# Two more weight pieces prepared ahead of the first step, rows copied ahead of the activation tables, reciprocals half a step later

## The chip, the cores and the metric

The kernel runs on one core of a Trainium2 chip. The metric is the device time of one execution in microseconds (us), lower is better. In the names used here PE is TensorE (matrix multiplies; PEld is its weight load), ACT is ScalarE, DVE is VectorE, POOL is GpSimd, and SP is the engine that issues the DMAs. Each engine works through its own queue in the order in which the program wrote it.

## The reference

Attention with two kinds of windows feeds a gated feed-forward layer. Only the shape of the work matters here:

```python
# q, k, v: batch 8, heads 8, seq 576, head_dim 64
scores = scale * q @ k.T            # masked to a window of 32 keys (plain, or every 4th key)
attn   = exp(scores - max) / (sum + 1e-9)
x      = attn @ v                   # as 4608 tokens x 512
h      = x @ w_in                   # 512 x 2048
sp     = max(h, 0) + log1p(exp(-abs(h)))
out    = (h * erf(sp)) @ w_out      # 2048 x 512
```

`w_in` and `w_out` come in as 64-bit numbers. The kernel turns each into a high and a low 32-bit part.

## The kernel before

**Attention units.** The attention is cut into 72 units of four blocks. Unit n passes through: `scores(n)` (PE), `mask_max(n)` (DVE: mask and row maximum), `exponents(n)` (four exponentials with row sums on ACT, then one small addition to the sums on POOL, line 207), `normalize(n)` (a reciprocal on DVE, then a multiplication of the unit's probabilities on POOL, line 212), `transposes(n)` (PE, line 217), `turned(n)` (a copy of the turned probabilities out of PSUM, line 220), `values(n)` (PE, line 233), `rows_hi(n)` (ACT casts the result into x's high part, line 266) and `rows_lo(n)` (DVE subtracts to get x's low part, line 271). A unit is transposed three units after it is scored (`LAG = 3`).

**Weights.** A piece of weights is loaded by a DMA, then passes ACT (`prep_act`, lines 369 and 374) and DVE (`prep_dve`, lines 383 to 389) over several calls. One call works on several pieces at once: on ACT a cast and one activation, on DVE four operations.

**Two parts.** First 14 visits, n = 0 to 13, run attention alone: visit n scores unit n and transposes unit n - 3 (`first_visit`). In visits 1 to `EARLY` a call on the weights goes along, and there the copy `turned` is on ACT; in the other visits it is on DVE. Then come steps t of two half steps x = 2t and 2t + 1. Each half step has `mm1` (PE, twelve 128x512 multiplies into `h`, line 446), `take` (DVE copies `h`), and from t = 2 also `mm2` (PE, twelve multiplies into `acc`, line 487) for the step two before. On ACT the odd half steps run `argument(t)` (sigmoid and logarithm with table loads, lines 458 and 459) and `table(t-1)` (erf, line 462). In x = 0 to 6 one unit n = 14 + x is scored in each half step and unit n - 3 = 11 + x is transposed. While t < 2 the transposes stand ahead of `mm1` in PE's queue; `values` and `scores` stand behind it.

All queues are written out by hand (a manual schedule): what the code says first on an engine runs first there.

Of the kernel before, what the change touches and what calls it, by code (L numbers as in the profile page):

```python
# [10 lines left out]
F32 = mybir.dt.float32  # L11
# [7 lines left out]
P = 128  # L19
# [15 lines left out]
PER = 4  # L35
# [18 lines left out]
SPC = FT // PAIR  # L54
# [5 lines left out]
USED = {p: min(t for t, (_, q, _) in enumerate(STEPS) if q == p) for p in range(SPC)}  # L60

LAG = 3
FIRST = NBLK + LAG + 2

FREE = FIRST - LAG + 4

EARLY = 9

SAVED = 2 * (HALF + 1) + 1

# [42 lines left out]
def attn_moe_kernel(ctx: ExitStack, tc: tile.TileContext, qk, v, masks, eye, w_in, w_out, out):  # L113
# [3 lines left out]
    def pool(name, bufs, space=bass.MemoryType.SB, **kw):  # L117
        return ctx.enter_context(tc.tile_pool(name=name, bufs=bufs, space=space, **kw))
# [7 lines left out]
    io, work, small = pool("io", 2), pool("work", 2), pool("small", 3)  # L126
# [47 lines left out]
    probs, maxes, sums, x_rows = {}, {}, {}, {}  # L174
# [3 lines left out]
    def scores(u):  # L178
        i = u % 2
        for j in range(PER):  # L180
            at, r = QW + key_start(u, j), j % 2 * BLK
            for h in range(2):
                hs = slice(h * D, (h + 1) * D)
                nc.tensor.matmul(sps[h][r:r + BLK, i, j // 2, :], qkz[i][hs, j * BLK:(j + 1) * BLK],  # L184
                                 qkz[i][hs, at:at + KEYS], start=True, stop=True)

    def mask_max(u):
        pr = probs[u] = work.tile([P, PER, KEYS], F32, name="prob", bufs=LAG + 1)
        nmax = maxes[u] = small.tile([P, PER], F32, name="nmax")
        for h in range(2):  # L190
            for p in range(PER // 2):
                n = PER * u + 2 * p
                nc.vector.tensor_tensor_reduce(  # L193
                    out=pr[:, 2 * h + p, :], in0=sps[h][:, u % 2, p, :], in1=mask[PAIRS.index((kind(n), kind(n + 1)))],
                    scale=-SCALE, scalar=BIG,
                    op0=ALU.add, op1=ALU.min, accum_out=nmax[:, 2 * h + p:2 * h + p + 1],
                )

    def exponents(u):
        nmax = maxes.pop(u)  # L200
        sums[u] = small.tile([P, PER], F32, name="ssum")
        for j in range(PER):
            nc.scalar.activation(  # L203
                out=probs[u][:, j, :], in_=probs[u][:, j, :], func=AF.Exp,
                scale=-1.0, bias=nmax[:, j:j + 1], accum_out=sums[u][:, j:j + 1],
            )
        nc.gpsimd.tensor_scalar(sums[u], sums[u], 1.0e-9, None, op0=ALU.add)

    def normalize(u):
        rinv = small.tile([P, PER], F32, name="rinv")  # L210
        nc.vector.reciprocal(out=rinv, in_=sums.pop(u))
        nc.gpsimd.tensor_tensor(probs[u], probs[u], rinv.broadcast_to([P, PER, KEYS]), op=ALU.mult)
# [9 lines left out]
    def turn(units):  # L222
        for u in units:
            transposes(u)
        for u in units:
            turned(u, nc.vector.tensor_copy)

    def values(u):
        xp, vt, pt = place(u), vz[u % 2], pz[u in second]
        for j in range(PER):  # L230
            r = j % 2 * BLK
            for h in range(2):
                nc.tensor.matmul(xp[h * D:(h + 1) * D, j * BLK:(j + 1) * BLK], vt[:, j, h, :],  # L233
                                 pt[:, 2 * h + j // 2, r:r + BLK], start=True, stop=True)

    def pieces(u):

# [26 lines left out]
    def rows_hi(u):  # L264
        for hi, _, src in rows_of(u):
            nc.scalar.copy(out=hi, in_=src)  # L266
# [27 lines left out]
    def has(u):  # L294
        return 0 <= u < NU

    def first_visit(n):

        m = n - LAG
        copy = nc.scalar.copy if 1 <= n <= EARLY else nc.vector.tensor_copy  # L300
        if has(m):
# [3 lines left out]
        if has(m):  # L305
            turned(m, copy)
        if 1 <= n <= EARLY:
            prep_act()
# [68 lines left out]
    def prep_dve(keep=None):  # L377

        if rest and rest[0][0] < calls[0]:
            _, w, hi, lo = rest.popleft()
            nc.vector.tensor_tensor(lo, w, hi.bitcast(F32), op=ALU.subtract)  # L383
        if begun and begun[0][0] < calls[0]:
            _, i, d, hi, lo, w = begun.popleft()
            t = w.bitcast(I32)
            nc.vector.tensor_scalar(t, t, 3, None, op0=ALU.logical_shift_left)
            nc.vector.scalar_tensor_tensor(t, d[:, :, 1], -0x80000000, t, op0=ALU.bitwise_and, op1=ALU.bitwise_or)  # L388
            nc.vector.scalar_tensor_tensor(t, d[:, :, 0], 29, t, op0=ALU.logical_shift_right, op1=ALU.bitwise_or)  # L389
            made.append((w, hi, lo))  # L390
            if i != keep:
                soon(load_w, i)
# [68 lines left out]
    def table(t):  # L461
        nc.scalar.activation(out=ls[t], in_=ls[t], func=AF.Erf, scale=-1.0)  # L462
# [66 lines left out]
    with tc.manual_schedule():  # L529
        load_qk(0)  # L530
        nc.sync.dma_start(out=cst, in_=masks)
        for t in vz:
            nc.gpsimd.memset(t[KEYS:P], 0.0)
        nc.gpsimd.memset(pz[0][KEYS:P], 0.0)
        load_qk(1)
        nc.sync.dma_start(out=ident, in_=eye)
        for n in range(FIRST):
            if n < 3:
                load_w(n)
            first_visit(n)  # L540
            if 1 <= n <= EARLY:
                prep_dve()
        normalize(FIRST - 2)
        rows_lo(FIRST - 1 - LAG)

        plan = visits()

        pause = 2 * (USED[SPC - 1] + 1) - 2

        late = 3  # L550
        todo, scaled = [], [FIRST - 1]
        for x in range(2 * (NT + 2)):
            t, j = divmod(x, 2)
            ns = plan.get(x, [])
            scored, ready = [n for n in ns if has(n)], [n - LAG for n in ns]
            second.update(ready[1:])

            if t < 2:
                turn(ready)
            if t < NT:  # L560
                after = STEPS[t + 1][0] if ends(t) and t + 1 < NT else None
                if x == 2 * HALF - 4:
                    load_x(1, range(twice))
                elif after and after > 1 and j == 0:
                    load_x(after, range(twice))
                if x in (2 * HALF - 2, SAVED):
                    hold(True)
                mm1(t, j)
                if x == 0:
                    for a in stores:  # L570
                        store_x(*a)
                if after is not None and j == PAIR - 1:
                    load_x(after, range(twice, CC))
                    hold(False)
                take(t, j)

            if j == 0 and x or x == 1:
                for u in todo:
                    exponents(u)
                scaled, todo = scaled + todo, []  # L580
            if j == 1 and 1 <= t <= NT:
                table(t - 1)
            if t >= 2:
                turn(ready)
            if j == 1 and 1 <= t <= NT:
                gate(t - 1, 0)
            if j == 0 and 2 <= t:
                gate(t - 2, 1)
            if j == 1 and t < NT:
                argument(t)  # L590
            if x != pause:
                prep_act()
            if x not in (pause, late):
                prep_dve(keep=2 if SAVED - 4 < x <= SAVED else None)
            if t >= 2:
                mm2(t - 2, j)
                if x == SAVED:
                    save()
                    hold(False)
                    load_w(2)  # L600
                elif ends(t - 2):
                    if j == 1:
                        store(STEPS[t - 2][0])
                    elif STEPS[t - 2][2] == 2:
                        fetch()
            for m in ready:
                values(m)
            for n in scored:
                scores(n)
            for n in ns:  # L610
                soon(load_qk, n + 2)
                soon(load_v, n - 1)
            for n in scored:
                mask_max(n)
                todo.append(n)
            if x == late:
                prep_dve()
            while scaled:
                normalize(scaled.pop(0))
            for m in ready:  # L620
                rows_hi(m)
            for m in ready:
                rows_lo(m)
            if x == SAVED + 2:
                nc.gpsimd.memset(pz[1][KEYS:P], 0.0)
        assert not todo and not prep and not staged and not begun and not made and not rest
# [84 lines left out]
```

## Time and profile before

| | |
|---|---|
| median of 3 runs | 943.51 us (941.78 to 943.67) |
| the profiled execution | 942.44 us, of which 940.7 us lie between its first and last instruction (the span) |
| PE busy in the span | 915.1 us, 97% |
| ACT, DVE, POOL busy | 642.5, 562.2, 82.9 us |
| mean granted TensorE clock | 0.997 of full speed |

Times of trace rows are microseconds from the span's start. A row of the timeline gives the start, the duration, the engine, the line and the operation; in brackets stands how long the engine had been idle and what it waited for.

### The profile page before, as it was taken

The numbers are of one execution on the slowest core, as the hardware profiler recorded it, in microseconds if no ns is written. First come the engines' busy times: TensorE is split into PE (matmuls) and PEld (weight loads), VectorE is DVE, ScalarE is ACT, GpSimd is POOL, SyncE is SP. The second block draws the span as 40 slices with busy tenths as digits, with TensorE's granted clock in tenths as the row PEclk, the third lists the DMA queues.
The fourth block names the chain that finished last, engine by engine and source line by source line (L and its number), as shares of the span: only waits on it lengthen the run. The fifth ranks groups of instructions, "written<-read, shape, count | busy, mean of one in ns | idle before, by whom it ended". The sixth has DMA issues, their size and how long they took to land.

```text
span 940.7 us, 15969 instructions
## 1 busy us (share of the span) xinstructions
PE 915.1 (97%) x6048; PEld 747.8 (80%) x6048; DVE 562.2 (60%) x1511; ACT 642.5 (68%) x1202; POOL 82.9 (9%) x154
## 2 busy tenths in 40 slices
PE   5789999999999999999999999999999999999998
PEld 4567887888888878888888878888888888888886
DVE  6879889886565545555665555555555444335434
ACT  7879888785866866667578657866566555445553
POOL 2321110110100100000000000100000000000000
PEclk9999999999999999999999999999999999999999
DMA  8766444432631242313232152314220302011001
GB/s 277 254 219 222 155 155 136 156 112 94 194 111 67 67 157 67 111 68 116 83 111 73 62 186 103 112 60 132 84 78 34 114 12 79 1 45 45 0 1 45
DMA packets 51500, 98.73 MB, mean 105 GB/s; under 512 B 7136, under 2 KB 20192, under 8 KB 51424
## 3 DMA queue, kind: packets, MB, share of 16 engines
q1 hardware_dynamic: 51136, 97.19, 30.9%
q8 instruction: 48, 0.79, 0.3%
q10 hardware_dynamic: 288, 0.52, 0.1%
q14 instruction: 28, 0.23, 0.1%
HBM read 69.52 MB, written 27.26 MB: 103 GB/s over the span
## 4 chain that ended last, share of the span: by engine, by line
PE 88%; DVE 6%; DMA 3%; ACT 2%; issue 1%; POOL 0%; SPq 0%; POOLq 0%; ACTq 0%; DVEq 0%
PE h L446 40%; PE acc L487 39%; PE tx L233 3%; PE sp L184 3%; PE sp L217 3%; DMA x<-xT 1%; DVE w L388 1%; DVE w L389 1%; DMA qk<-in_qk_dram 1%; DVE prob L193 1%; DVE win_lo L383 1%; PE acc L217 1%; DVE s L469 1%; DMA dbl<-in_w_in_dram 0%; DVE pT L220 0%
## 5 line engine op out<-in xcount | busy, mean ns | idle before, releaser
L454 DVE COPY hc<-h 128x512 f32<-128x512 f32 x144 | 99.5, 691 | 273.5 <-PE h L446 273.1
L446 PE MATMUL h<-x,win_hi 128*128 128x512 f32 x832 | 259.3, 393 | 0.9 <-DMA x<-xT 0.9
L487 PE MATMUL acc<-wout_hi,ghi 128*128 128x512 f32 x576 | 227.5, 395 | 1.2 <-DVE rows L271 1.0
L487 PE MATMUL acc<-wout_lo,ghi 128*128 128x512 f32 x576 | 224.4, 390 | 0.0
L458 ACT ACTIVATE s<-hc 128x1024 f32<-128x1024 f32 x72 | 76.4, 1062 | 184.4 <-DVE hc L454 184.3
L446 PEld LDWEIGHTS h<-x,win_hi 128*128 128x128 f32 x832 | 155.0, 188 | 35.2 <-issue 1.4
L446 PE MATMUL h<-x,win_lo 128*128 128x512 f32 x416 | 162.3, 390 | 0.0
L487 PE MATMUL acc<-wout_hi,glo 128*128 128x512 f32 x576 | 158.8, 389 | 0.0
L487 PEld LDWEIGHTS acc<-wout_hi,ghi 128*128 128x128 f32 x576 | 108.2, 188 | 23.6 <-DVE rows L271 1.4
L487 PEld LDWEIGHTS acc<-wout_hi,glo 128*128 128x128 f32 x576 | 108.1, 188 | 22.6
L487 PEld LDWEIGHTS acc<-wout_lo,ghi 128*128 128x128 f32 x576 | 108.3, 188 | 21.4
L203 ACT ACTIVATE prob<-prob,nmax 128x96 f32<-128x96 f32 x288 | 104.0, 364 | 5.4 <-DVE nmax L193 5.1
L473 DVE TENSOR_TENSOR glo<-s,ghi 128x512 fp32r<-128x512 f32 x144 | 99.7, 693 | 5.1
L459 ACT ACT_TABLE_LOAD x72 | 92.4, 1283 | 1.3
L462 ACT ACT_TABLE_LOAD x72 | 92.4, 1283 | 1.3
L469 DVE TENSOR_TENSOR s<-hc,s 128x1024 f32<-128x1024 f32 x72 | 88.1, 1224 | 7.1 <-ACT s L462 7.1
L446 PEld LDWEIGHTS h<-x,win_lo 128*128 128x128 f32 x416 | 78.3, 188 | 16.7
L193 DVE CUSTOM_DVE_ANT_0 prob<-sp,cst 128x96 f32<-128x96 f32 x288 | 54.8, 253 | 51.8 <-PE sp L184 51.7
L446 PE MATMUL h<-dbl,win_hi 128*128 128x512 f32 x256 | 80.7, 396 | 0.0
L266 ACT CAST rows<-tx 128x64 fp32r<-128x64 f32 (+5 forms) x116 | 26.2, 356 | 75.2 <-PE tx L233 75.2
L462 ACT ACTIVATE s<-s 128x1024 f32<-128x1024 f32 x72 | 76.5, 1062 | 0.8
L459 ACT ACTIVATE s<-s 128x1024 f32<-128x1024 f32 x72 | 76.4, 1061 | 0.8
(59 smaller groups left out, 929.2 us busy)
## 6 DMA issues: line engine op xcount, KB each, us to landing
xT<-rows SPq DMA_DIRECT2D x26, 576.0 KB, 4.7
v<-in_v_dram SPq DMA_DIRECT2D x72, 192.0 KB, 3.8
qk<-in_qk_dram SPq DMA_DIRECT2D x48, 272.0 KB, 3.9
dbl<-in_w_in_dram SPq DMA_DIRECT2D x16, 512.0 KB, 4.2
dbl<-in_w_out_dram SPq DMA_DIRECT2D x16, 512.0 KB, 3.4
qk<-in_qk_dram SPq DMA_DIRECT2D x24, 288.0 KB, 3.9
out_dram<-w SPq DMA_DIRECT2D x26, 256.0 KB, 2.3
x<-xT SPq DMA_DIRECT2D x8, 320.0 KB, 5.2
```

The lines of the kernel that those rows point to most:

```text
L184: nc.tensor.matmul(sps[h][r:r + BLK, i, j // 2, :], qkz[i][hs, j * BLK:(j + 1) * BLK], qkz[i][hs, at:at + KEYS], start=True, stop=True)
L193: nc.vector.tensor_tensor_reduce(out=pr[:, 2 * h + p, :], in0=sps[h][:, u % 2, p, :], in1=mask[PAIRS.index((kind(n), kind(n + 1)))], scale ...
L203: nc.scalar.activation(out=probs[u][:, j, :], in_=probs[u][:, j, :], func=AF.Exp, scale=-1.0, bias=nmax[:, j:j + 1], accum_out=sums[u][:, ...
L217: nc.tensor.transpose(out=turn_place(u)[0:KEYS, j * P:(j + 1) * P], in_=pr[:, j, :], identity=ident)
L446: nc.tensor.matmul(h, w[:, cc, ft * P:(ft + 1) * P], x[cc], start=(k == 0 and i == 0), stop=(k == CC - 1 and i == 2))
L454: nc.vector.tensor_copy(out=hs[t][:, j], in_=h)
L458: nc.scalar.activation(out=ls[t], in_=hs[t], func=AF.Sigmoid, scale=-1.0)
L459: nc.scalar.activation(out=ls[t], in_=ls[t], func=AF.Ln, bias=TINY)
L462: nc.scalar.activation(out=ls[t], in_=ls[t], func=AF.Erf, scale=-1.0)
L469: nc.vector.tensor_tensor(out=e, in0=hc, in1=e, op=ALU.mult)
L473: nc.vector.tensor_tensor(out=glo, in0=e[:, j], in1=ghi.bitcast(F32), op=ALU.subtract)
L487: nc.tensor.matmul(acc[tt], g[:, tt * P:(tt + 1) * P], w[:, ft, :], start=(first and w is wout_hi and g is ghi), stop=(last and g is glo))
```

## The change

`EARLY` goes from 9 to 11, so visits 10 and 11 each get a call on the weights, and their `turned` copy moves from DVE to ACT. In return half steps 2 and 3 have no such call. In the half steps before t = 2, `values`, `scores` and `rows_hi` are written ahead of `argument` and `prep_act` (`attend`). `normalize` of a unit whose exponentials were issued in half step x is written in half step x + 1, behind `take` and ahead of `gate`, unless its transposes come in x + 1: then it stays at the end of x. Two small buffers get one more copy.

```diff
-EARLY = 9
+EARLY = 11
...
-        sums[u] = small.tile([P, PER], F32, name="ssum")
+        sums[u] = small.tile([P, PER], F32, name="ssum", bufs=LAG + 1)
...
+    def attend(ready, scored):
+        for u in ready:
+            values(u)
+        for u in scored:
+            scores(u)
+        for u in ready:
+            rows_hi(u)
...
-        pause = 2 * (USED[SPC - 1] + 1) - 2
-        late = 3
-        todo, scaled = [], [FIRST - 1]
+        pause = 2, 3, 2 * (USED[SPC - 1] + 1) - 2
+        due = {n - LAG: x for x, ns in plan.items() for n in ns}
+        todo, scaled, fresh = [], [FIRST - 1], []
...
-                scaled, todo = scaled + todo, []
+                fresh, todo = todo, []
             if j == 1 and 1 <= t <= NT:
                 table(t - 1)
+            if t < 2:
+                attend(ready, scored)
             if t >= 2:
                 turn(ready)
+            while scaled:
+                normalize(scaled.pop(0))
+            scaled, fresh = fresh, []
...
-            if x != pause:
+            if x not in pause:
                 prep_act()
-            if x not in (pause, late):
                 prep_dve(keep=2 if SAVED - 4 < x <= SAVED else None)
...
-            for m in ready:
-                values(m)
-            for n in scored:
-                scores(n)
+            if t >= 2:
+                attend(ready, scored)
...
-            if x == late:
-                prep_dve()
-            while scaled:
-                normalize(scaled.pop(0))
-            for m in ready:
-                rows_hi(m)
+            for u in [u for u in scaled if due[u] == x + 1]:
+                scaled.remove(u)
+                normalize(u)
             for m in ready:
                 rows_lo(m)
```

Three places show the move in the queues. The first is POOL's queue from the last visit to half step 3. Line 207 is the addition to a unit's sums and line 212 the multiplication of its probabilities; the tile numbers of before are prob_666, 708, 778 and 846 for units 12, 13, 14 and 15, whose sums for 14 and 15 are ssum_811 and 877. Before:

```order
L212 TENSOR_TENSOR prob_666<-prob_666,rinv_723 128x384
L212 TENSOR_TENSOR prob_708<-prob_708,rinv_784 128x384
L207 TENSOR_SCALAR ssum_811<-ssum_811 128x4
L212 TENSOR_TENSOR prob_778<-prob_778,rinv_852 128x384
L207 TENSOR_SCALAR ssum_877<-ssum_877 128x4
L212 TENSOR_TENSOR prob_846<-prob_846,rinv_916 128x384
```

In the changed kernel the same units are prob_684, 726, 802 and 865, and the sums of 14 and 15 are ssum_829 and 892:

```order
L212 TENSOR_TENSOR prob_684<-prob_684,rinv_741 128x384
L212 TENSOR_TENSOR prob_726<-prob_726,rinv_788 128x384
L207 TENSOR_SCALAR ssum_829<-ssum_829 128x4
L207 TENSOR_SCALAR ssum_892<-ssum_892 128x4
L212 TENSOR_TENSOR prob_802<-prob_802,rinv_917 128x384
L212 TENSOR_TENSOR prob_865<-prob_865,rinv_969 128x384
```

The multiplication of unit 14 stood ahead of the addition of unit 15 and now stands behind it.

The second place is ACT's queue from the exponentials of unit 14 to those of unit 15 (half steps 1 and 2). `rows` is x's part, `s` and `hc` belong to `argument(0)`, `wout_hi` and `w` to the weights. Before:

```order
L203 ACTIVATE prob_778,ssum_811<-prob_778,nmax_779 128x96 x4
L458 ACT_TABLE_LOAD
L458 ACTIVATE s_749<-hc_748 128x1024
L459 ACT_TABLE_LOAD
L459 ACTIVATE s_749<-s_749 128x1024
L369 CAST wout_hi_82<-w_516 128x512
L374 ACTIVATE w_820<-dbl1_552 128x512
L266 CAST rows_788<-acc1_94 128x256
L203 ACT_TABLE_LOAD
L203 ACTIVATE prob_846,ssum_877<-prob_846,nmax_847 128x96 x4
```

In the changed kernel:

```order
L203 ACTIVATE prob_802,ssum_829<-prob_802,nmax_803 128x96 x4
L274 CAST rows_786<-acc1_94 128x256
L466 ACT_TABLE_LOAD
L466 ACTIVATE s_767<-hc_766 128x1024
L467 ACT_TABLE_LOAD
L467 ACTIVATE s_767<-s_767 128x1024
L377 CAST wout_hi_82<-w_622 128x512
L382 ACTIVATE w_855<-dbl0_657 128x512
L203 ACT_TABLE_LOAD
L203 ACTIVATE prob_865,ssum_892<-prob_865,nmax_866 128x96 x4
```

The cast of x's part (unit 12) moved ahead of `argument(0)`; the exponentials of unit 15 stay behind `argument(0)` and the call on the weights.

The third place is PE's queue at the start of half step 3, in the changed kernel: the transposes of unit 14 (prob_802), then `mm1`, then `values(14)`.

```order
L217 MATMUL acc3_96<-ident_58,prob_802 96x128 x4
L454 MATMUL h_109<-x0_97,win_hi_80 128x512 x2
L454 MATMUL h_109<-x0_97,win_lo_81 128x512
L454 MATMUL h_109<-x1_98,win_hi_80 128x512 x2
L454 MATMUL h_109<-x1_98,win_lo_81 128x512
L454 MATMUL h_109<-x2_99,win_hi_80 128x512 x2
```

Nothing moved here: PE's queue holds the same operations in the same order in both kernels, from the first to the last.

## Rows read from the trace of the kernel before

**Rows 1.** Busy time by stretch: length, PE, PEld, DVE, ACT, POOL, clock, DMA.
```profile
0.00:49.60 49.60, 34.27 (x447) 25.16 (x448) 37.50 (x179) 37.57 (x151) 14.75 (x32) 1.00 0.78 259
49.60:90.00 40.40, 35.54 (x317) 27.28 (x316) 33.47 (x101) 35.20 (x82) 8.03 (x11) 0.96 0.67 224
90.00:941.00 851.00, 845.27 (x5287) 695.39 (x5285) 491.23 (x1233) 569.70 (x972) 60.14 (x111) 1.00 0.27 90
```

**Rows 2.** Timeline, half steps 1 to 3, all engines.
```profile
57.60 0.69 PE L233 MATMUL acc<-pT,v 128*64 128x64 f32 x16 [0.51 <-DVE pT L220]
57.63 1.28 ACT L458 ACT_TABLE_LOAD   x1
...
63.33 0.36 ACT L266 CAST rows<-acc 128x256 fp32r<-128x256 f32 x1
...
64.79 0.69 PE L233 MATMUL acc<-pT,v 128*64 128x64 f32 x16 [2.71 <-DVE pT L220]
...
66.25 1.09 PE L217 MATMUL acc<-ident,prob 128*96 128x128 f32 x4
...
66.44 0.60 ACT L369 CAST wout_hi<-w 128x512 fp32r<-128x512 f32 x1
...
70.77 0.69 PE L233 MATMUL acc<-pT,v 128*64 128x64 f32 x16
```

**Rows 3.** Busy time by stretch, PE's low clock (columns as in Rows 1).
```profile
66.00:68.00 2.00, 2.00 (x16) 1.55 (x12) 1.93 (x8) 2.00 (x8) 0.76 (x1) 0.50 0.05 12
68.00:70.00 2.00, 2.00 (x9) 1.61 (x8) 1.58 (x10) 1.97 (x3) 0.83 (x1) 0.81 0.57 215
```

**Rows 4.** PE's waits, 60 to 90 us: total, times, longest.
```profile
PE acc L487 <- DVE rows L271: 1.0, 1, 1.0
PE sp L217 <- POOL prob L212: 0.7, 1, 0.7
```

**Rows 5.** Timeline, visits 9 and 10.
```profile
34.25 0.57 ACT L220 COPY pT<-acc 96x512 f32<-96x512 f32 x1
34.34 0.17 DVE L211 RECIPROCAL rinv<-ssum 128x4 f32<-128x4 f32 x1
...
34.88 1.12 PE L233 MATMUL acc<-pT,v 128*64 128x64 f32 x16 [0.68 <-ACT pT L220]
...
35.77 0.67 DVE L383 TENSOR_TENSOR win_lo<-w,win_hi 128x512 fp32r<-128x512 f32 x1
...
37.62 0.37 ACT L203 ACTIVATE prob<-prob,nmax 128x96 f32<-128x96 f32 x1
...
38.15 0.68 DVE L220 COPY pT<-acc 96x512 f32<-96x512 f32 x1
...
38.88 1.12 PE L233 MATMUL acc<-pT,v 128*64 128x64 f32 x16 [0.55 <-DVE pT L220]
```

**Rows 6.** Timeline of PE, visits 11 to 13 and half step 0.
```profile
40.49 1.09 PE L217 MATMUL acc<-ident,prob 128*96 128x128 f32 x4 [0.48 <-POOL prob L212]
...
41.50 0.92 PE L184 MATMUL sp<-qk 64*64 64x96 f32 x16
...
46.80 0.64 PE L217 MATMUL acc<-ident,prob 128*96 128x128 f32 x4 [0.83 <-POOL prob L212]
...
49.28 0.64 PE L217 MATMUL acc<-ident,prob 128*96 128x128 f32 x4 [0.38 <-POOL prob L212]
49.65 0.30 PEld L446 LDWEIGHTS h<-x,win_hi 128*128 128x128 f32 x2
...
52.59 0.69 PE L233 MATMUL acc<-pT,v 128*64 128x64 f32 x16
```

**Rows 7.** Timeline of DVE and POOL, last visit and half step 0.
```profile
49.19 0.16 DVE L211 RECIPROCAL rinv<-ssum 128x4 f32<-128x4 f32 x1
...
50.92 0.22 POOL L207 TENSOR_SCALAR ssum<-ssum 128x4 f32<-128x4 f32 x1 [1.70 <-ACT prob L203]
...
51.22 0.83 POOL L212 TENSOR_TENSOR prob<-prob,rinv 128x384 f32<-128x384 f32 x1
```

More of the change, by code (lines that the diff above doesn't have):

```diff
@@ L188, in mask_max @@
         pr = probs[u] = work.tile([P, PER, KEYS], F32, name="prob", bufs=LAG + 1)
-        nmax = maxes[u] = small.tile([P, PER], F32, name="nmax")
+        nmax = maxes[u] = small.tile([P, PER], F32, name="nmax", bufs=LAG + 1)
         for h in range(2):
@@ L575, in attn_moe_kernel @@
                 take(t, j)
-            if j == 0 and x or x == 1:
+            if x == 1 or j == 0 and x:
                 for u in todo:
                     exponents(u)
-                scaled, todo = scaled + todo, []
+                fresh, todo = todo, []
             if j == 1 and 1 <= t <= NT:
                 table(t - 1)
+            if t < 2:
+                attend(ready, scored)
             if t >= 2:
                 turn(ready)
+            while scaled:
+                normalize(scaled.pop(0))
+            scaled, fresh = fresh, []
             if j == 1 and 1 <= t <= NT:
```

## The prediction

> **What bounds the kernel now.** I first read the busy times by stretch [rows 1]. From 90 us to the end PE is busy 845.27 of 851.00 us: there the kernel is bound by PE, and since the change leaves PE's queue as it is, operation for operation, nothing can be won or lost there except by a new wait. The time that can move lies ahead of 90 us: PE is idle 15.3 us in the visits (49.60 - 34.27) and 4.9 us in the first half steps (40.40 - 35.54). So the forecast is the answer to one question: how much earlier or later does PE come out of this stretch?
>
> The timeline shows the largest wait of the half steps [rows 2]. `argument(0)` starts on ACT at 57.63, and with the call on the weights behind it holds ACT until 63.33. Only then comes the cast of x's part of unit 12. DVE's subtraction needs it, the copy of the next unit's turned probabilities is queued behind that subtraction, and `values(13)` on PE starts at 64.79 after 2.71 us idle. [...] Two more waits follow, 1.0 us of `mm2` for x's low part and 0.7 us of transposes for a POOL multiplication [rows 4].
>
> **Term 1, two more pieces in the visits.** In visit 9 DVE goes from the reciprocal at 34.34 to the piece at 35.77 (1.43 us for reciprocal, mask and low parts) and to the next copy at 38.15: a call on the weights holds DVE 2.38 us [rows 5]. Visits 10 and 11 get that, and lose the copy of about 0.6 us, so DVE's queue grows by 3.6 us in all. That is the upper bound. The lower: ACT starts the exponentials of visit 9 at 37.62, four of about 0.36 us, so it can copy only from 39.05 where DVE copied at 38.15; `values` follow a copy on ACT by 0.63 (34.25 to 34.88), so they start at 39.68 and not 38.88: 0.8 us [rows 5].
>
> The value between: after `values(7)` (1.12 us) the transposes of visit 11 start at 40.8 instead of 40.49, and its scores, which end 1.93 us behind that start (41.50 + 0.92 - 40.49), end at 42.7 [rows 6]. DVE then has mask and low parts (about 1.4) and the piece (2.4) until 46.5, the copy of unit 9 (0.6) and the reciprocal. The multiplication starts 0.3 later, at 47.4, takes 0.83 [rows 7], and the transposes of unit 10 start at 48.3 instead of 46.80. The next visit adds some 0.3, since ACT, with four more operations in the two visits, is late with its exponentials as well: transposes of unit 11 at 51.1 instead of 49.28, first `mm1` at 51.5 instead of 49.65 [rows 6]. I take **+1.8 us** (0.8 to 3.6).
>
> **Term 2, the clock in the visits.** The windows print no change of clock there, but the same sixteen small multiplies of `values` last 1.12 us at 38.88 and 0.69 at 57.60, and transposes 1.09 at 40.49 and 0.64 at 46.80 [rows 2, 5, 6]; 1.09 is also what transposes last at 66.25, where 0.50 is granted [rows 2, 3]. PE thus ran at the lower level through the visits with weights and rose in the first ones without. With two more such visits, and PE waiting in them, it rises later: nothing if in the same place, up to 2.1 us if only within the first `mm1` (transposes, scores and values of two visits at 0.4 us more each where they are not hidden by a wait, and half of an `mm1` of 2.94, from 49.65 to 52.59). I take **+0.5** (0 to 2.1), since the last two visits without weights should lift it.
>
> **Term 3, from the first mm1 to the transposes of unit 14.** `values(12)` started 7.95 us after the first `mm1` (57.60 - 49.65), and DVE and PE have the same work up to there, so now 51.5 + 7.95 = 59.4. The cast of x's part follows when they end (0.69), at 60.15, and lasts 0.36. It is now ahead of `argument(0)`, so the subtraction on DVE finds it done, and `values(13)` start right behind `mm1`: that ended at 62.08 (64.79 - 2.71) and ends 1.85 later now, at 63.9. The wait of 2.71 us is gone. But ACT now starts `argument(0)` at 60.5 and not at 57.63. It and the weights take 5.70 (57.63 to 63.33), until 66.2; the exponentials of unit 15 with their table load take 2.75 (63.33 + 0.36 to 66.44), until 68.95 [rows 2].
>
> POOL's queue now has the addition of unit 15 ahead of the multiplication of unit 14, as the change's rows show. The trace shows what that does: the reciprocal for unit 12 was there at 49.19, its multiplication ran only at 51.22, right behind the addition of unit 13, which had waited 1.70 us for ACT [rows 7]. So addition at 69.1, multiplication 0.30 later at 69.4, over at 70.3. The transposes of unit 14 wait for it, and in PE's queue the whole fourth `mm1` stands behind them. PE has had nothing since `values(13)` (0.69) and scores (some 0.6), 65.2: **a new wait of 5.1 us**, in place of 2.71. The transposes start at 70.3 instead of 66.25: +4.05, of which 1.8 is term 1. **+2.25 us.** DVE's reciprocal of unit 14 moved too, but at 65 it has nothing to wait for, and the calls left out of half steps 2 and 3 free DVE and ACT only while PE waits for POOL.
>
> [...]
>
> **Term 4, behind the wait.** From these transposes to `values(14)` it took 4.52 us (66.25 to 70.77) [rows 2], most of it at the lower clock. After a longer wait the clock will be low again, so I take the same stretch: **0**. Bounds: all at the higher level (0.37 for transposes, 49.28 to 49.65, and 2.94 for `mm1` [rows 6]: 3.31) it is -1.2; all at the lower twice that, 6.6: +2.1.
>
> **Term 5, later waits.** PE arrives over 4 us later, DVE has one call on the weights (2.4 us) less ahead of `mm2` and ACT one less as well: the waits of 1.0 and 0.7 us [rows 4] should be hidden. **-1.65** (0 to -2.3, with the small issue gaps beside them).
>
> **Moved at no cost.** Behind half step 4 the reciprocals go at most one half step later, on DVE behind `take`, with PE's `mm1` and `mm2` of that half step (2.94 us for one such set of twelve multiplies) as cover; their multiplications are needed a half step after that, or are left where they were by the rule on due units. On SP two loads of 512 KB are issued in visits 10 and 11 and not in half steps 2 and 3; they are wanted two calls later. If that cover were gone, a transposition would wait up to one multiplication, 0.83 us, at a time.
>
> **Sum.** 1.8 + 0.5 + 2.25 + 0 - 1.65 = +2.9 us on the profiled 942.44: 945.3. The median of the runs shown is 1.07 above that execution; I count about half of this and forecast **945.9 us**, 0.25% above the median. About 0.2% (1.9 us) is what a measurement of this kernel can tell from no change.
>
> **Rivals.**
> - *The clock costs more.* It stays low into the first `mm1` (term 2 at 2.1) and through the fourth (term 4 at +1.0): +5.5, 948.5. For it: long waits in both places. Against: it rose while `mm1` ran after 66.25. Chance 0.12.
> - *The costs are small and the exchange is even.* Term 1 at its lower bound, term 2 at 0: +1.4, 944. For it: PE waited 0.48 to 0.83 us before the transposes of visits 11 to 13, so not all of what comes late costs. Against: those waits are for the same chain that grows [rows 6]. With term 4 at its lower end it is about zero. Chance 0.28.
> - *Faster: the multiplication of unit 14 is not held.* Then the 2.71 us are won, the slow stretch is gone (4.52 - 3.31 = 1.2), and term 5 comes too (1.65), against +1.8: -3.75, 938.7. What decides is when the exponentials of unit 15 end on ACT: each us by which they end before 68.95 is won, and from about 64, five us earlier, the wait is gone. For it: only a shorter `argument`; against: its table loads and 1024-wide operations are the same instructions. Chance 0.12.
> - *The change doesn't do what it says*, and `values(13)` waits as before: only if x's cast came late in spite of the new order; within the chances above.
>
> **Chances and range.** The forecast (+1.9 to +5, 944.5 to 948.5) has 0.48. Slower by over 0.2%: 0.48 and 0.12. Within 0.2%: 0.28. Faster: 0.12. The range leaves out the faster rival and the far end of the bounds: 942.3 to 949.
>
> **What would show it.** After: first `mm1` near 51.5 (term 1); sixteen multiplies at 1.1 us up to some point past 45 (term 2); no wait of `values` for DVE's copy near 64; a wait of PE's transposes for POOL's multiplication of about 5 us near 65 to 70, with ACT's exponentials ending just before it; a granted clock of 0.50 behind it; no wait of `mm2` for line 279. I am wrong if that wait for POOL is under 2 us, or if the visits take no longer.

## Result and the profile after

| | before | after |
|---|---|---|
| median | 942.65 us (940.93 to 944.76, 7 runs) | 947.16 us (945.75 to 947.77, 7 runs) |
| ratio, 95% interval | | 1.0044 (1.0031 to 1.0057) |
| the profiled execution | 942.44 us, span 940.7 | 947.37 us, span 945.6 |

The changed kernel is 0.44% slower: 4.5 us by the medians, 4.9 us by the two profiled executions. The forecast was 945.9 us, which is 2.4 us above the median of the three runs shown with the kernel before (943.51).

The busy times come first. This is the first part of the page of the changed kernel (busy us, share of the span, number of instructions):

```profile
PE 917.9 (97%) x6048; PEld 749.5 (79%) x6048; DVE 581.6 (62%) x1509; ACT 643.3 (68%) x1204; POOL 109.3 (12%) x154
```

ACT's sum has hardly moved. DVE is busy 19 us longer and POOL 26 us longer, with no work added in all: the weights' calls only changed places. That was not forecast, and it is followed up below (e6).

The same stretches as in [rows 1], for the changed kernel:

```profile
0.00:49.60 49.60, 35.06 (x439) 25.82 (x440) 39.45 (x179) 40.16 (x153) 14.08 (x32) 1.00 0.82 277
49.60:90.00 40.40, 33.49 (x287) 25.92 (x286) 27.89 (x93) 29.69 (x73) 8.47 (x12) 0.92 0.60 200
90.00:946.00 856.00, 849.33 (x5329) 697.74 (x5327) 514.24 (x1239) 573.47 (x979) 86.71 (x112) 1.00 0.27 90
```

Between 49.6 and 90 us PE is busy 2.05 us less than before and issues 30 multiplies fewer, and its granted clock there is 0.92, not 0.96. Behind 90 us PE is still busy all but 6.7 of 856 us. So most of the loss lies ahead of 90 us; what lies behind is sized further below.

The timeline of the changed kernel from half step 0 to half step 3, all engines, shows where:

```profile
51.08 0.31 PEld L454 LDWEIGHTS h<-x,win_hi 128*128 128x128 f32 x2
...
59.68 0.69 PE L233 MATMUL acc<-pT,v 128*64 128x64 f32 x16 [1.14 <-DVE pT L220]
...
60.80 1.28 ACT L466 ACT_TABLE_LOAD   x1
...
64.33 0.69 PE L233 MATMUL acc<-pT,v 128*64 128x64 f32 x16
...
64.83 0.17 DVE L211 RECIPROCAL rinv<-ssum 128x4 f32<-128x4 f32 x1
64.94 0.56 PE L184 MATMUL sp<-qk 64*64 64x96 f32 x16
65.43 0.60 ACT L377 CAST wout_hi<-w 128x512 fp32r<-128x512 f32 x1
...
66.61 1.28 ACT L203 ACT_TABLE_LOAD   x1
...
69.00 0.36 ACT L203 ACTIVATE prob<-prob,nmax 128x96 f32<-128x96 f32 x1
...
69.60 0.22 POOL L207 TENSOR_SCALAR ssum<-ssum 128x4 f32<-128x4 f32 x1 [9.26 <-ACT rows L274]
69.90 0.83 POOL L212 TENSOR_TENSOR prob<-prob,rinv 128x384 f32<-128x384 f32 x1
...
70.78 1.09 PE L217 MATMUL acc<-ident,prob 128*96 128x128 f32 x4 [5.28 <-POOL prob L212]
...
76.06 0.69 PE L233 MATMUL acc<-pT,v 128*64 128x64 f32 x16
```

Read it from the bottom. PE stood 5.28 us before the transposes of unit 14, for POOL's multiplication of line 212. The reciprocal that this multiplication needs was there at 65.00 (64.83 + 0.17), but POOL started it at 69.90, right behind the addition of unit 15 (line 207 at 69.60). That addition had to wait for the last exponential of unit 15 (69.00 + 0.36; the bracket names what ACT had next, the cast of line 274, but that cast ends only at 69.88, when the addition is over). This exponential stands on ACT behind `argument(0)` (from 60.80), a call on the weights (from 65.43) and a table load. The wait of 2.71 us of [rows 2] is gone: `values(13)` run at 64.33. PE's waits of over 0.2 us between 60 and 90 us (total, times, longest) are now this one alone; those of [rows 4] are gone:

```profile
PE acc L217 <- POOL prob L212: 5.3, 1, 5.3
```

The granted clock behind the wait (the number ahead of the DMA share), PE alone, to be held against [rows 3]:

```profile
66.00:68.00 2.00, 0.00 (x0) 1.00 0.93 299
68.00:70.00 2.00, 0.00 (x0) 0.54 0.30 104
70.00:72.00 2.00, 1.22 (x5) 0.50 0.50 210
72.00:74.00 2.00, 2.00 (x6) 0.50 0.21 85
74.00:76.00 2.00, 2.00 (x8) 0.76 0.00 0
```

It fell while PE stood, so that, taking it as either 1.00 or 0.50, some 2.6 us at 0.50 were spent on no work at all (1.84 of the two us at a mean of 0.54, and 0.78 more until 70.78), and it was back at about 75 us (0.76 from 74 to 76).

How far the changed kernel is behind is best followed at one instruction that every half step has, DVE's copy of `h` (`take`). It is 1.46 us late in half step 0, 5.30 in half step 3, 3.47 in half step 7, and 4.93 in the last. Three of its rows (half steps 3, 4 and 7 of the changed kernel; before, they started at 70.87, 77.53 and 98.89):

```profile
76.17 0.69 DVE L462 COPY hc<-h 128x512 f32<-128x512 f32 x1 [3.58 <-PE h L454]
...
81.02 0.69 DVE L462 COPY hc<-h 128x512 f32<-128x512 f32 x1
...
102.36 0.69 DVE L462 COPY hc<-h 128x512 f32<-128x512 f32 x1 [0.77 <-PE h L454]
```

### The profile page after: what moved, and what is told of

It is laid out like the page before. It is cut to its first block, busy times and chain, and to the rows that moved or that the text cites. A ratio compares the mean times of both kernels' runs of the same rounds, so it can differ in the third digit from the quotient of the medians.

```text
span 945.6 us, 15964 instructions
## 1 busy us (share of the span) xinstructions
PE 917.9 (97%) x6048; PEld 749.5 (79%) x6048; DVE 581.6 (62%) x1509; ACT 643.3 (68%) x1204; POOL 109.3 (12%) x154
## 4 chain that ended last, share of the span: by engine, by line
PE 89%; DVE 5%; DMA 2%; ACT 2%; issue 1%; POOL 0%; SPq 0%; POOLq 0%; DVEq 0%
PE h L454 40%; PE acc L495 39%; PE tx L233 3%; PE sp L184 3%; PE sp L217 3%; DMA x<-xT 1%; DVE w L396 1%; DVE w L397 1%; DMA qk<-in_qk_dram 1%; DVE win_lo L391 1%; DVE prob L193 1%; DVE w L395 0%; DMA dbl<-in_w_in_dram 0%; PE acc L217 0%; DVE x L279 0%
## 5 line engine op out<-in xcount | busy, mean ns | idle before, releaser
L481 DVE TENSOR_TENSOR glo<-s,ghi 128x512 fp32r<-128x512 f32 x144 | 107.8, 749 | 5.2
L212 POOL TENSOR_TENSOR prob<-prob,rinv 128x384 f32<-128x384 f32 x72 | 86.2, 1208 | 113.4 <-DVE rinv L211 104.4
L207 POOL TENSOR_SCALAR ssum<-ssum 128x4 f32<-128x4 f32 x72 | 20.3, 282 | 496.2 <-ACT prob L203 485.2
```

The costliest lines, as they stand in the source:

```text
L481: nc.vector.tensor_tensor(out=glo, in0=e[:, j], in1=ghi.bitcast(F32), op=ALU.subtract)
```

## Experiments

My theory (A): the loss is the wait of the transposes of unit 14 for POOL, which the later multiplications make. The rivals: (B) the two pieces moved into the visits cost it; (C) multiplications written half a step later run beside DVE's wide operations everywhere, and the sum of these delays costs it. Ratios are to the kernel before, with a 95% interval, from 6 to 12 runs of each kernel beside 23 or 35 of the kernel before.

### e1: unit 14 alone back in its half step

In the changed kernel, unit 14 is normalized at the end of half step 1, ahead of unit 15's addition; every other unit stays as changed.

```diff
-            for u in [u for u in scaled if due[u] == x + 1]:
+            for u in [u for u in scaled if due[u] == x + 1 or x == 1]:
```

> The changed kernel with one unit's normalize put back: unit 14 is normalized at the end of half step 1, so its multiplication stands ahead of the addition of unit 15 on POOL again; all other moves stay. Theory A (the loss is the wait of the transposes of unit 14 for POOL, 5.28 us, and the low clock behind it): the wait is gone, the transposes start right behind the scores near 65.5 us, and the next thing that is late is the copy for values(14), about 2 us behind ACT's cast of x's part of unit 13; in all 4 to 5 us faster than the changed kernel, within 1.5 us of the kernel before. Rival B (the price lies in the two pieces in the visits): the wait is gone but the gain is under 2 us, and it stays 3 us or more above the kernel before. Rival C (what costs is that reciprocals half a step later make POOL's multiplications run beside DVE's wide operations in every half step): under 1 us of gain, since only one unit moved.

Measured: 944.15 us, ratio 1.0009 (0.9998 to 1.0020). With one unit's multiplication put back, 3 of the 4.5 us are back. PE's timeline of e1:

```profile
71.73 0.69 PE L233 MATMUL acc<-pT,v 128*64 128x64 f32 x16 [2.25 <-DVE pT L220]
```

The wait of 5.28 us is gone, and in this execution the clock stayed at 1.00 from 66 to 76 us. That is not so in every run of e1: its mean clock is 1.000 in three of the twelve runs (941.5 to 942.5 us), this one among them, and lower in the others (what this tells stands in the last section). Part of the wait came up again, 2.25 us, one link on: now `values(14)` wait for the copy of the turned probabilities on DVE, which stands behind work that waits for ACT's cast behind the exponentials of unit 15. A holds as the main cause, but the gain is about 3 us and not the 4 to 5 that were expected; B and C as they were put (a gain of under 2 us, and of under 1 us) do not hold.

### e2: all units back in their half step

The changed kernel with every normalize at the end of its own half step, as before the change.

```diff
-                fresh, todo = todo, []
+                scaled, todo = scaled + todo, []
...
-            while scaled:
-                normalize(scaled.pop(0))
-            scaled, fresh = fresh, []
...
-            for u in [u for u in scaled if due[u] == x + 1]:
-                scaled.remove(u)
-                normalize(u)
+            while scaled:
+                normalize(scaled.pop(0))
```

> The changed kernel with all of normalize where it was in the kernel before (end of the half step of the exponentials); the pieces and the earlier rows stay. Theory A: as with unit 14 alone, within 0.7 us of that kernel. Rival C: 1 us or more faster than the kernel with unit 14 alone put back, and POOL's multiplications back from 1.21 us to about 0.83 us each. Rival B: 3 us or more above the kernel before.

Measured: 942.49 us, ratio 1.0002 (0.9991 to 1.0014): no change to the kernel before. So the moved pieces and the early x parts together win and lose nothing that can be measured (from 0.9 us faster to 1.3 us slower), and the later multiplications make the changed kernel slower. Between e1 and e2 the intervals overlap, so this pair doesn't decide on C. PE's timeline of e2 has the same leftover wait as e1's:

```profile
71.50 0.97 PE L233 MATMUL acc<-pT,v 128*64 128x64 f32 x16 [2.25 <-DVE pT L220]
```

### e3: x's parts early, nothing else

The kernel before, with `attend` for t < 2 alone (its definition, as in the change, is left out here).

```diff
...
+            if t < 2:
+                attend(ready, scored)
             if t >= 2:
                 turn(ready)
...
-            for m in ready:
-                values(m)
-            for n in scored:
-                scores(n)
+            if t >= 2:
+                attend(ready, scored)
...
-            for m in ready:
-                rows_hi(m)
```

> The kernel before with one part of the change alone: values, scores and the cast of x's part ahead of argument and the weights in half steps 0 to 3; nine pieces, normalize as before. Theory A: the wait of values(13), 2.71 us, is gone and the transposes of unit 14 do not wait, but values(14) waits about 2 us for the copy behind the next cast, and mm2 waits longer for x's low part (1.0 us before, 2 to 3 us now): 0.5 to 2 us faster than the kernel before. Rival: the wait of 2.71 us is hidden anyway by what comes behind it, no difference within 0.5 us.

Measured: 942.31 us, ratio 0.9994 (0.9984 to 1.0004). I had expected a gain of 0.5 to 2 us; it may be nothing. PE's timeline of e3 says why:

```profile
63.83 0.69 PE L233 MATMUL acc<-pT,v 128*64 128x64 f32 x16 [0.20 <-DVE pT L220]
...
70.96 0.69 PE L233 MATMUL acc<-pT,v 128*64 128x64 f32 x16 [2.62 <-DVE pT L220]
...
78.94 0.50 PE L495 MATMUL acc<-wout_hi,ghi 128*128 128x512 f32 x1 [1.30 <-DVE rows L279]
```

The wait of `values(13)`, 2.71 us in [rows 2], is down to 0.20, and `values(14)` wait 2.62 us in its place. The edit does what it says, and the wait goes to the next unit: ACT's chain of `argument(0)` and the exponentials of unit 15 starts later, because x's cast, which has to wait for `values(12)`, now stands ahead of it (in the changed kernel, which has this order too, the cast runs at 60.41 and `argument(0)` at 60.80, against 57.63 in [rows 2]).

### e4: the two pieces, nothing else

The kernel before with the calls on the weights moved.

```diff
-EARLY = 9
+EARLY = 11
...
-        pause = 2 * (USED[SPC - 1] + 1) - 2
+        pause = 2, 3, 2 * (USED[SPC - 1] + 1) - 2
...
-            if x != pause:
+            if x not in pause:
                 prep_act()
-            if x not in (pause, late):
                 prep_dve(keep=2 if SAVED - 4 < x <= SAVED else None)
...
-            if x == late:
-                prep_dve()
```

> The kernel before with the other part alone: eleven pieces ahead of the first step, none in half steps 2 and 3; rows and normalize as before. Theory A: the first mm1 starts 1.4 us later, values(13) waits as before, and the waits of mm2 and of transposes behind it shrink from 1.7 us to under 1 us: within 1.5 us of the kernel before. Rival B: 2.5 us or more slower than the kernel before.

Measured: 943.29 us, ratio 1.0010 (0.9997 to 1.0022): B costs 0.8 us by the medians, with an interval that just takes in nothing. PE's timeline of e4:

```profile
66.28 0.69 PE L233 MATMUL acc<-pT,v 128*64 128x64 f32 x16 [3.00 <-DVE pT L220]
...
84.34 0.64 PE L217 MATMUL sp<-ident,prob 128*96 128x128 f32 x4 [0.64 <-POOL prob L212]
```

The wait of `mm2` for x's low part ([rows 4], 1.0 us) is gone, because DVE has no call on the weights in half steps 2 and 3. What the visits lose is mostly given back there.

### e5: the later multiplications, nothing else

The kernel before, with the edit that defers `normalize` alone. The lines that give two small buffers one more copy and set up `due` and `fresh` are left out here.

```diff
...
-                scaled, todo = scaled + todo, []
+                fresh, todo = todo, []
...
+            while scaled:
+                normalize(scaled.pop(0))
+            scaled, fresh = fresh, []
...
-            while scaled:
-                normalize(scaled.pop(0))
+            for u in [u for u in scaled if due[u] == x + 1]:
+                scaled.remove(u)
+                normalize(u)
```

> The kernel before with the third part of the change alone: normalize half a step later; nine pieces, the cast of x's part behind argument and the weights as before. Theory A: POOL now has the addition of unit 15 ahead of the multiplication of unit 14; ACT's exponentials of unit 15 end about 66.5 us as before, so the transposes of unit 14 wait near 66 to 68 us for POOL, 1.5 to 2.5 us, behind the wait of 2.7 us of values(13) that stays; part of it is given back by shorter later waits: 0.5 to 3 us slower than the kernel before. Rival C (the half step's delay costs by POOL's multiplications beside DVE's wide operations everywhere): as much from the half steps behind the fourth alone as here. A third reading, that the delay is harmless without the earlier cast: no difference within 0.5 us.

Measured: 948.79 us, ratio 1.0060 (1.0045 to 1.0074). The direction is A's; the size, 6.0 us, is twice my upper end. PE's timeline of e5:

```profile
66.09 0.69 PE L233 MATMUL acc<-pT,v 128*64 128x64 f32 x16 [2.74 <-DVE pT L220]
...
69.82 1.09 PE L217 MATMUL acc<-ident,prob 128*96 128x128 f32 x4 [2.56 <-POOL prob L212]
...
83.15 0.50 PE L487 MATMUL acc<-wout_hi,ghi 128*128 128x512 f32 x1 [1.28 <-DVE rows L271]
...
89.56 0.64 PE L217 MATMUL sp<-ident,prob 128*96 128x128 f32 x4 [0.70 <-POOL prob L212]
```

The old wait (2.71 in [rows 2]) and the new one stand behind each other, 2.74 and 2.56 us. I had thought that PE's lag would hide the later waits of [rows 4]; they stay, 1.28 and 0.70. In the changed kernel, and in e4, the one of `mm2` is gone, so it is the weights' calls that were taken out of half steps 2 and 3 which take it away, and not the lag. The one of the transposes stays in e3 (0.69), e4 (0.64) and e5 (0.70) and is gone in e2, which has hardly any lag: there it is the other two edits together. The granted clock of e5 behind the two waits, PE alone:

```profile
70.00:72.00 2.00, 2.00 (x8) 0.50 0.94 296
72.00:74.00 2.00, 2.00 (x6) 0.50 0.96 316
74.00:76.00 2.00, 2.00 (x15) 0.69 0.45 183
```

From the transposes to `values(14)` it takes 5.85 us (75.67 - 69.82), where 4.52 was the figure before. So without the other two edits the deferral costs more than the whole change, and those edits give back some 1.5 us of it.

### e6: the later multiplications from half step 4 on

As e5, but the first four half steps keep the old place of `normalize`. This is C alone. The lines that are the same as in e5 are left out.

```diff
...
+            if x >= 4:
+                while scaled:
+                    normalize(scaled.pop(0))
+            scaled, fresh = scaled + fresh, []
...
-            while scaled:
-                normalize(scaled.pop(0))
+            for u in [u for u in scaled if due[u] == x + 1 or x < 4]:
+                scaled.remove(u)
+                normalize(u)
```

> The kernel before with normalize half a step later from half step 4 on only, so units 13 to 15 are as before. POOL's multiplications now start beside DVE's wide operations of the gate: their mean goes from 0.83 to about 1.2 us and the gate's casts and subtractions on DVE get longer. Theory A: PE waits for neither of these there, no difference within 1 us. Rival C: 1.5 us or more slower than the kernel before.

Measured: 943.17 us, ratio 1.0002 (0.9991 to 1.0013). C falls as the cause of the 4.5 us. The multiplications do get longer. The durations of POOL's multiplications (ns, shortest, median, longest; first and last start), for the kernel before, then e6, then the changed kernel:

```profile
L212 POOL TENSOR_TENSOR prob<-prob,rinv x72: 827/828/1112, 10.2 to 711.4; 128x384 f32<-128x384 f32 x72
```

```profile
L212 POOL TENSOR_TENSOR prob<-prob,rinv x72: 825/1005/1810, 9.9 to 713.8; 128x384 f32<-128x384 f32 x72
```

```profile
L212 POOL TENSOR_TENSOR prob<-prob,rinv x72: 825/1006/1808, 10.4 to 719.6; 128x384 f32<-128x384 f32 x72
```

The median goes from 0.83 to 1.005 us: this is where the 26 us of POOL went. Most of it is paid by idle time, but not all, and the lags of `take` against the kernel before show what isn't. From half step 7 to half step 15 e6 falls back by 0.62 us (from 1.49 ahead to 0.87 ahead), and so do the four other kernels that defer the multiplications there: 0.66 (changed), 0.60 (e1), 0.84 (e5), 0.63 (e7). The four that don't defer them move by -0.39 (e2), -0.07 (e3), 0 (e4) and +0.13 (b1). So C seems to have a price, 0.6 to 0.8 us in those eight half steps by one execution of each kernel, too small for the interval of e6's time. No other stretch has one that recurs.

### e7: the pause moved from half step 2 to half step 1

In the changed kernel the call on the weights that stood behind `argument(0)` is left out, and half step 2 has one.

```diff
-        pause = 2, 3, 2 * (USED[SPC - 1] + 1) - 2
+        pause = 1, 3, 2 * (USED[SPC - 1] + 1) - 2
```

> The changed kernel with the call on the weights of half step 1 moved to half step 2, so ACT has about 1.2 us less between argument(0) and the exponentials of unit 15, and the sum of the work is the same. Theory A: the wait of the transposes of unit 14 for POOL shrinks by about that, from 5.28 to 4.1 us, and the kernel is 0.5 to 1.5 us faster than the changed one. Rival B: the wait may shrink, the time stays within 0.3 us of the changed kernel.

Measured: 946.65 us, ratio 1.0040 (1.0025 to 1.0055). PE's timeline of e7:

```profile
69.88 1.09 PE L217 MATMUL acc<-ident,prob 128*96 128x128 f32 x4 [4.43 <-POOL prob L212]
```

The wait is 4.43 instead of 5.28 us, shorter by 0.85 of the 1.18 us that ACT spent on the weights there (65.43 to 66.61 in the changed kernel): A's chain runs through ACT as forecast. In the total the two kernels can't be told apart, so the gain of 0.5 to 1.5 us that A expected is neither shown nor excluded.

### b1: both the old and the new wait taken away

In the changed kernel, only unit 15 is deferred; in half step 2 `attend` stands ahead of the exponentials, so that x's cast of unit 13 is early too; in half step 3 x's low part is subtracted ahead of `gate` (DVE's product of `h` with ACT's result, and its split into a high and a low part).

```diff
-        todo, scaled, fresh = [], [FIRST - 1], []
+        todo, scaled, fresh = [], [], [FIRST - 1]
...
+            if x == 2:
+                attend(ready, scored)
             if x == 1 or j == 0 and x:
                 for u in todo:
                     exponents(u)
-                fresh, todo = todo, []
+                fresh, todo = fresh + todo, []
...
-            if t < 2:
+            if t < 2 and x != 2:
                 attend(ready, scored)
...
+            if x == 3:
+                for m in ready:
+                    rows_lo(m)
...
-            for u in [u for u in scaled if due[u] == x + 1]:
+            for u in [u for u in scaled if due[u] == x + 1 or x != 2]:
                 scaled.remove(u)
                 normalize(u)
-            for m in ready:
+            for m in ready if x != 3 else []:
                 rows_lo(m)
```

> A version meant to be faster than both kernels: the changed kernel with normalize at the end of the half step of the exponentials except for unit 15, whose reciprocal stays behind take of half step 3; in half step 2 the cast of x's part of unit 13 ahead of the exponentials of unit 15; in half step 3 the subtraction for unit 14 ahead of the gate. Theory A: no wait of transposes(14) for POOL, and the wait of 2.25 us of values(14) for DVE's copy, which was left when only unit 14 was put back, is gone as well, since DVE no longer stands behind the exponentials of unit 15; then mm2 waits about 1 to 2 us for the gate, so about 1 to 2 us faster than the kernel before. Rival: that last wait takes all of it, within 0.5 us of the kernel before.

Measured: 943.57 us, ratio 1.0008 (0.9993 to 1.0023): the 1 to 2 us that I expected to win did not come. PE's timeline of b1:

```profile
65.23 0.69 PE L233 MATMUL acc<-pT,v 128*64 128x64 f32 x16 [0.18 <-DVE pT L220]
...
77.27 0.61 PE L217 MATMUL sp<-ident,prob 128*96 128x128 f32 x4 [3.46 <-DVE nmax L193]
```

The two waits are gone, and the transposes of unit 15 wait 3.46 us for DVE's mask (line 193), which has to free the buffer into which they go (`sp` in the row) and is now queued behind the subtraction and the gate, which wait for ACT's erf and the cast behind it (erf at 72.07, cast at 73.04, subtraction at 73.70 after 2.43 us idle, mask at 76.69). It is again a wait that ACT causes, for the third time, each time one link further down. What ACT has to do in these half steps (`argument(0)`, the exponentials of unit 15, the erf) is late whatever stands between, as far as these kernels show. Work was taken off ACT there only in e7, one call that came back behind the exponentials, and the wait shrank by 0.85 us.

## Why the prediction was right, and where its sizes were off

The sign, the place and the mechanism were right: a new wait of PE's transposes of unit 14 for POOL, forecast at 5.1 us and measured at 5.28, in place of the wait of 2.71 us. That the total came within 1.3 us of the measured one is in part luck: terms 1 and 2 were 0.87 us too dear and term 3 was 0.85 us too cheap, and these two errors cancel. The loss that was forecast, 2.4 us over the three runs known then, is about half of the 4.5 us measured. The parts, from the two profiled executions:

| | forecast | measured |
|---|---|---|
| terms 1 and 2: first `mm1` | +2.3 | +1.43 (51.08 - 49.65) |
| term 3: from there to the transposes of unit 14 | +2.25 | +3.10 (19.70 - 16.60) |
| term 4: on to `values(14)` | 0 | +0.76 (5.28 - 4.52) |
| term 5: waits hidden up to half step 7 | -1.65 | -1.83 (3.47 - 5.30) |
| behind half step 7 | 0 | +1.46 (4.93 - 3.47) |
| sum | +2.9 | +4.9 |

The first four rows end at 3.46, the lag of half step 7 (3.47).

*Terms 1 and 2* were too dear, and one profile is not enough to size them. The transposes of half step 0 start at 48.78 to 50.81 us in the four profiles with nine early pieces (mean 49.69) and at 50.41 to 52.22 in the six with eleven (mean 51.16), 1.47 us later. So the pieces cost about 1.5 us in all. The split into a term for DVE's queue (1.8) and one for the clock (0.5) does not come out of the traces. Up to the first `mm1` PE is busy 36.26 us and idle 14.82 (before: 34.32 and 15.33), so it is the same 448 multiplies that last longer; over the ten profiles the mean busy time rises by 1.1 us and the idle time by 0.4. The multiplies are slow for longer, as term 2 said; that the clock makes them so is not shown: the granted clock reads 1.00 up to 49.6 us in both kernels, and from 50 to 54 us in the changed one. PE's timeline of the changed kernel, last visit and half step 0:

```profile
49.01 1.12 PE L233 MATMUL acc<-pT,v 128*64 128x64 f32 x16
...
50.41 0.95 PE L217 MATMUL acc<-ident,prob 128*96 128x128 f32 x4 [0.28 <-POOL prob L212]
...
54.04 0.69 PE L233 MATMUL acc<-pT,v 128*64 128x64 f32 x16
```

The sixteen multiplies of 49.01 still last 1.12 us and those of 54.04 only 0.69, while before the transposes were at 0.64 from 46.80 on [rows 6].

*Term 3* was the mis-sized one, by 0.85 us. The step that failed is "DVE and PE have the same work up to there": `values(12)` start 8.60 us behind the first `mm1` (59.68 - 51.08), not 7.95. The reciprocal of unit 13 moved as well, so POOL's multiplication of that unit ran beside a wide DVE operation. The timeline of the changed kernel, DVE and POOL, half step 0:

```profile
54.76 0.17 DVE L211 RECIPROCAL rinv<-ssum 128x4 f32<-128x4 f32 x1
...
55.07 1.12 POOL L212 TENSOR_TENSOR prob<-prob,rinv 128x384 f32<-128x384 f32 x1 [1.79 <-DVE rinv L211]
55.42 1.05 DVE L395 TENSOR_SCALAR w<-w 128x512 int32<-128x512 int32 x1
```

In the kernel before the two ran apart:

```profile
53.90 0.42 DVE L387 TENSOR_SCALAR w<-w 128x512 int32<-128x512 int32 x1
...
56.72 0.83 POOL L212 TENSOR_TENSOR prob<-prob,rinv 128x384 f32<-128x384 f32 x1 [4.67 <-DVE rows L271]
```

DVE's operation took 1.05 us instead of 0.42, and that 0.63 is what `values(12)` are late by. It ended 0.28 us behind POOL's (56.47 and 56.19), which took 1.12 instead of 0.83; why both took longer no run here shows. The other 0.2 us of term 3 lie on ACT, between the start of `argument(0)` and the transposes (9.98 us, where the forecast had 9.8).

*Term 4* came within its bounds, but taking the old stretch was 0.76 us too cheap. That the clock would be low again held (0.50 from 70 to 74 us); it was low for longer, from the wait itself to about 75 us.

*Term 5* held in size: no PE wait of 0.4 us or more is left from 71 to 90 us. Of the two reasons given, e4 and e5 show which one ended `mm2`'s wait: it is the weights' calls that are gone (no such wait in e4), not the lag (1.28 us in e5).

*Behind half step 7*, which I put at nothing ("Moved at no cost"), the changed kernel loses 1.46 us. 0.66 of it lies between half steps 7 and 15 and belongs to the deferred multiplications (e6): there the cover named for them was not whole. Another 0.70 comes between half steps 40 and 50, where `mm1` waits 0.79 us for loads of x (0.43 before). In that stretch the eight experiments move by -0.79 to +0.53 us, those of them with the deferral by -0.77 to -0.04, so nothing shows that the change causes it.

*The rivals.* The clock's rival (948.5) lies about as near to the measured 947.16 as the forecast. Of its two places it had the second nearly right: the clock was low through most of the fourth `mm1` (0.50 from 70 to 74 us), for +0.76 us of its +1.0. The first it had wrong: the first `mm1` ran as fast as before, from 51.08 to the `values` at 54.04, 2.96 us against 2.94, with a granted clock of 1.00 from 50 to 54 us. The rest of the loss came with other terms. The even exchange (+1.4) had terms 1 and 2 nearer than the forecast (0.8, measured 1.43), and fell by terms 3 and 4 and what lies behind half step 7. The faster rival needed unit 14's multiplication not to be held, and e1 does this to the kernel: the wait goes, as it said, but 944.15 and not 938.7 is what remains. The slow stretch is gone in e1's profile (one of three runs in twelve), but "the 2.71 us are won" was wrong: e3 and e1 show that wait again at `values(14)`, 2.62 and 2.25 us.

## What to carry to other kernels

Here a late input was carried to what stood behind it in the queue: POOL had unit 14's reciprocal at 65.00 and started its multiplication at 69.90, behind the addition of unit 15. Before a small operation is moved, look up what now stands ahead of it and what that waits for. Several waits in a row hung on one engine that is late (ACT), and taking away one of them moved it to the next link: 2.71 us of `values(13)` became 2.62 of `values(14)` in e3, 5.28 of the transposes of unit 14 became 2.25 of `values(14)` in e1, and in b1, without either, the transposes of unit 15 wait 3.46. Follow such a chain to its last link before counting the wait as a gain. To price a change of several edits, run each alone as well: here one edit cost 6.0 us by itself, the other two together nothing that can be measured, and all three 4.5.

## What the hardware showed that was not expected

- **A wait and the clock.** The granted clock fell to 0.50 behind PE waits of 2.25 us (e2), 2.71 (before), 3.00 (e4), 4.43 (e7) and 5.28 (after), and behind the two of e5 (2.74 and 2.56). It stayed at 1.00 up to 76 us behind waits of 2.25 (e1), 2.62 (e3) and 2.67 (e6), and in b1 behind the longer one of 3.46, from 73.81 to 77.27. The granted clock of b1, PE alone:

```profile
74.00:76.00 2.00, 0.00 (x0) 1.00 0.77 211
76.00:78.00 2.00, 0.73 (x6) 1.00 0.74 229
78.00:80.00 2.00, 2.00 (x10) 1.00 0.21 78
```

So between 2.25 and 3.46 us the length of the wait alone does not tell which way it goes.

- **What the fall costs.** In the ten profiles the mean granted clock of a run tells whether it happened: the six with the fall have 0.996 to 0.998, the four without (e1, e3, e6, b1) 0.999 or 1.000. Of the runs of the kernel before that were made beside the experiments, 35 have a mean of 0.996 to 0.998, with 943.2 us on average, and 15 have 0.999 or 1.000, with 941.8. That is 1.4 us that goes with the fall, give or take 0.65 (95%). In the changed kernel, e5 and e7 none of the 19 runs has a mean above 0.998 (one lies at 0.978), so as far as the mean tells the clock fell in each of them. A part of the loss is this; my estimate is 0.4 us (15 of 50 runs of the kernel before escape the 1.4 us). Eight more runs lie at 0.980 to 0.991 with 941.7 us; where their clock fell is not shown.
- **POOL beside DVE.** The 128x384 multiplication took 0.83 us in the median before, and 1.01, up to 1.81, where it was written later; DVE's 128x512 TENSOR_SCALAR took 1.05 instead of 0.42 beside it. In all it is 26 us more on POOL and 19 on DVE; in e6, which has this edit alone and from half step 4 on, POOL is busy 107.9 us (82.9 before) and DVE 581.3 (562.2). In half steps 7 to 15 0.6 to 0.8 us of it reach PE.
- **The visits vary.** The first 50 us of the same program differ by up to 2 us between two kernels that are alike there (the transposes of half step 0 start at 48.78 in e6 and 50.81 in e3), so a term of one or two microseconds there can't be read from one pair of profiles.
